# Moving the sums of y to GpSimd, new planner costs for VectorE, and a float64 conversion by 256 columns with its results in place

## The chip, the cores and the metric

The kernel runs on one NeuronCore of one Trainium2 chip. The metric is the device time of one execution in microseconds (us). The names of the engines are those of the profile: PE is TensorE (PEld its weight loads), DVE is VectorE, ACT is ScalarE, POOL is GpSimd, SP is SyncE, which only issues DMAs here. Every engine works its own queue in order: an instruction that waits holds up all that stand behind it in its queue.

## The reference, cut to what matters

Three stages follow each other: a delta-rule attention, a soft mixture of eight experts, and a two-branch product with two more matrices.

```python
y = attention(q, k, v, beta)            # 4 x 8 heads, 768 tokens, state 48 x 48
x = y laid out as (3072, 384)
P = sinkhorn(exp(x @ w_gate))           # (3072, 8)
for e in range(8):                      # w1: (8, 384, 1024)  w2: (8, 1024, 384)
    h = np.maximum(x @ w1[e], 0.0)
    out += P[:, e:e+1] * (h @ w2[e])
a = out @ W1; b = out @ W2              # these weights are float64
result = ((a * b) @ W3) @ W_out         # (3072, 384)
```

## The kernel before

All products are made in three PE passes on split operands: a float32 operand is kept as a high part (rounded by ACT to the PE's fp32r format) and a low part (operand minus high part, also fp32r), and a product is high·high + high·low + low·high. So for each tile of weights and each tile of activations somebody makes a high part (ACT) and a low part (a subtraction, on DVE or POOL).

The program has three phases. Phase A (0 to about 510 us) is the attention with expert 0 beside it. Phase B (to about 1916 us) does experts 1 to 7 for all tokens: three passes over two chunks of 512 tokens, and in each pass 7 experts times 2 halves of the hidden width. One such half is a *unit*; there are 42. Phase C does the last two stages with the converted float64 weights. The change touches phase B alone, and the conversion that runs beside it.

A unit (method `unit`) is 138 matmuls of 128x512: 66 for `x @ w1`, in a scheme in the manner of Strassen that needs sums of weights and sums of token chunks, and 72 for `h @ w2`. The results of the first part come out of PSUM by `hold` (ACT copies a partial sum into `rt`) and `done` (DVE adds PSUM to `rt`, ACT makes the rectified high part `hB` or `hA`, DVE the low part). The second part makes six results y. DVE multiplies each y in PSUM by its expert's probabilities into `tmp` (a ring of two buffers), and a second instruction adds `tmp` to `acc`. That addition is what the title calls the sum of y.

While a unit runs, `load_pair` prepares the weights of the next one, two pairs per unit: four DMAs bring a pair into `rawB` (two buffers, so that one pair fills it), ACT makes the high parts (`wA`, 768 and 640 columns), DVE or POOL the low parts, then five small sums of 128 columns are made within `rawB`, and of three of the sums again high and low parts (`wS`, 256 columns twice, and `wA`, 128 columns). Only then is `rawB` free for the next pair's DMAs.

The float64 weights of the last stage are converted on the way (`convert`), at the lowest priority: by jobs of `CN` columns a DMA brings the raw words into `cvr`, DVE and ACT take exponent and mantissa apart into `cv`, two instructions of DVE or POOL put them together, DVE clears what is too small, ACT makes the high part and DVE or POOL the low part, in `cvs`, and two DMAs store these into DRAM (`w1_d`, `w2_d`, `wo_d`, `w3_d`). There is one `cv` and one `cvs`.

After the fourth expert's first half in each pass, `add_first` brings in expert 0's results from DRAM: six instructions multiply them by the probabilities in `tmp`, six add them to `acc`.

The order of all of it is made by a planner (class `Plan`). Every operation gets a priority, the engines that may do it, and a cost on each. The planner plays the program through with these costs and emits the instructions in that order. Where two engines may do an operation it takes the one that would end it first, where DVE's cost counts 1.5 times (`BIAS`). So a cost is not only a length: it decides the engine and each later place in the queues. `act(n)`, `dve(n)` and `pool2(n)` are the costs in us for n columns; `pool2` is `(2.2 * n + 70) / 1000`.

## Time and profile before

| | us |
|---|---|
| median of three runs | 2279.29 (2276.01 to 2284.38) |
| the profiled execution's own time | 2278.97 |
| its span, first to last instruction | 2277.2 |

The profile is of one execution, and all durations below come from it. The span is 1.77 us shorter than that execution's own time. Busy shares over the whole span are PE 94%, PEld 80%, DVE 73%, ACT 38%, POOL 25%. These are averages over phases with different limits: in phase B DVE is at 82 to 89%, in phase C at a quarter. So the phases are read apart, by stretches of time.

### The profile page before, as it was taken

Reading aid. Unit: us, or ns where it says so; the run is one execution under the profiler, and the core shown is the slowest. Engines: PE = TensorE matmul, PEld = TensorE weight load, DVE = VectorE, ACT = ScalarE, POOL = GpSimd, SP = SyncE. Lnnn points to the kernel's source line nnn. Section 1 sums busy time; section 2 is a strip of 40 time slices with the busy share of each in tenths; the row PEclk is TensorE's granted clock in tenths of the full one; section 3 lists DMA queues with packets and bytes.
Section 4 is the critical chain, followed back from the end, with each engine's and each line's share of the span. In section 5 each row is a group of like instructions: output and inputs, shape, how many; then the busy total and the mean of one; then the engine's idle time right before and its main releaser. Section 6 shows DMA issues by size and latency. Waiting matters only on the chain.

```text
span 2277.2 us, 41249 instructions
## 1 busy us (share of the span) xinstructions
PE 2148.3 (94%) x16017; PEld 1812.5 (80%) x16017; DVE 1653.9 (73%) x3128; ACT 864.6 (38%) x1795; POOL 568.3 (25%) x682
## 2 busy tenths in 40 slices
PE   3989999989999999999999999999999999999999
PEld 3989999987777777777777777777777888888888
DVE  7667866678898999988889989989978666122211
ACT  3333233344434444444434444445433432122222
POOL 3000000033333433343234423423323222300000
PEclk6899999999999999999999999999999999999999
DMA  5331232143224333342323232432322215600000
GB/s 190 90 89 46 86 93 60 32 120 111 82 84 130 93 98 87 89 135 79 92 81 111 84 100 84 131 94 79 88 83 72 65 51 166 134 28 28 15 14 28
DMA packets 228132, 194.90 MB, mean 86 GB/s; under 512 B 17056, under 2 KB 211552, under 8 KB 227168
## 3 DMA queue, kind: packets, MB, share of 16 engines
...
q8 instruction: 125, 2.05, 0.4%
...
## 4 chain that ended last, share of the span: by engine, by line
PE 54%; DVE 22%; issue 8%; DMA 7%; ACT 5%; POOL 3%; SPq 1%; DVEq 0%; POOLq 0%; ACTq 0%
PE b L323 54%; DMA rawB<-in_moe_w 4%; DVE wA L334 2%; DVE hB L337 2%; DVE rt L334 2%; DVE hA L337 2%; DVE cv L337 2%; DVE tmp L334 2%; DVE acc L334 2%; DVE rawB L334 1%; SPq L354 1%; ACT wA L327 1%; DVE wS L334 1%; DVE cv L1192 1%; DVE cv L1196 1%
## 5 line engine op out<-in xcount | busy, mean ns | idle before, releaser
L323 PE MATMUL b<-hB,wA 128*128 128x512 f32 x2277 | 587.9, 398 | 9.2 <-DVE hB L337 9.2
L323 PEld LDWEIGHTS b<-hB,wA 128*128 128x128 f32 x2277 | 429.9, 189 | 119.9 <-DVE hB L337 17.9
L323 PE MATMUL b<-hA,wA 128*128 128x256 f32 (+1 forms) x1611 | 334.2, 338 | 21.1 <-DVE hA L337 19.5
L334 DVE TENSOR_TENSOR rt<-b,rt 128x512 f32<-128x512 f32 x300 | 202.7, 684 | 192.1 <-PE b L323 190.3
L323 PE MATMUL b<-xr,wA 128*128 128x256 f32 (+1 forms) x1620 | 322.0, 336 | 0.0
L323 PEld LDWEIGHTS b<-hA,wA 128*128 128x128 f32 x1611 | 248.5, 191 | 65.8 <-DVE hA L337 31.7
L323 PEld LDWEIGHTS b<-xr,wA 128*128 128x128 f32 x1620 | 251.3, 192 | 32.1
L334 POOL TENSOR_TENSOR wA<-rawB,wA 128x640 fp32r<-128x640 f32 (+2 forms) x117 | 161.2, 1377 | 389.2 <-ACT wA L327 320.5
L323 PE MATMUL b<-xT,wA 128*128 128x512 f32 x1008 | 250.5, 390 | 0.0
L327 ACT ACTIVATE rt<-b 128x512 f32<-128x512 f32 x300 | 176.4, 592 | 139.2 <-PE b L323 122.2
L323 PEld LDWEIGHTS b<-xT,wA 128*128 128x128 f32 x1008 | 189.1, 188 | 40.7
L327 ACT ACTIVATE wA<-rawB 128x768 fp32r<-128x768 f32 (+2 forms) x252 | 155.7, 624 | 147.1 <-PE b L323 76.4
L323 PE MATMUL b<-xT,wS 128*128 128x512 f32 x756 | 204.8, 397 | 7.0 <-ACT wS L327 2.7
L334 DVE TENSOR_TENSOR tmp<-b,pb 128x512 f32<-128x512 f32 x234 | 160.5, 686 | 64.4 <-PE b L323 62.3
L334 DVE TENSOR_TENSOR acc<-acc,tmp 128x512 f32<-128x512 f32 x240 | 180.9, 754 | 4.9
L323 PEld LDWEIGHTS b<-xT,wS 128*128 128x128 f32 x756 | 143.5, 190 | 41.4 <-ACT wS L327 3.6
L327 ACT ACTIVATE cvs<-cv 128x128 fp32r<-128x128 f32 x136 | 42.2, 310 | 349.3 <-DVE cv L337 329.3
L337 DVE SCALAR_TENSOR_TENSOR hB<-rt,hB 128x512 fp32r<-128x512 f32 x170 | 146.8, 868 | 21.4 <-ACT hB L1009 19.6
L334 POOL TENSOR_TENSOR rawB<-rawB 128x128 f32<-128x128 f32 x224 | 132.9, 596 | 108.7 <-DVE rawB L334 51.9
L1009 ACT ACTIVATE hB<-rt 128x512 fp32r<-128x512 f32 x170 | 106.3, 629 | 89.4 <-DVE rt L334 87.8
L334 POOL TENSOR_TENSOR cv<-cv 128x128 f32<-128x128 f32 x118 | 72.9, 618 | 220.9 <-DVE cv L1196 136.3
L334 DVE TENSOR_TENSOR wA<-rawB,wA 128x768 fp32r<-128x768 f32 (+2 forms) x135 | 114.2, 846 | 18.4 <-ACT wA L327 17.5
...
## 6 DMA issues: line engine op xcount, KB each, us to landing
...
w_d<-cvs SPq DMA_DIRECT2D x224, 64.0 KB, 2.3
...
```

The costliest lines, as they stand in the source:

```text
L323: self.nc.tensor.matmul(*args, skip_group_check=True, **kw)
L327: self.nc.scalar.activation(out=out, in_=in_, func=AF.Copy, **({} if scale is None else {"scale": scale}))
L334: self.E[eng].tensor_tensor(out=out, in0=in0, in1=in1, op=op)
L337: self.nc.vector.scalar_tensor_tensor(out=out, in0=in0, scalar=scalar, in1=in1, op0=op0, op1=op1)
L354: return self.g.op({eng: cost}, lambda _: e.dma_start(out=out(), in_=in_()), r=r, w=w, prio=prio, nbytes=nbytes, lat=lat)
L1009: g.op({"ACT": act(512)}, lambda e: nc.scalar.activation(out=hv(0), in_=tv(), func=AF.Relu), r=[t], w=[(out, 0, 0)], prio=pe)
L1192: g.op({"DVE": dve(m)}, lambda e, f=f, rv=rv: ts(out=f(), in0=rv()[:, :, 1], scalar1=3, scalar2=0x3FFFFFF8, op0=ALU.logical_shift_left, op ...
L1196: g.op({"DVE": dve(m, 2)}, lambda e, f=f, ee=ee: ts(out=ee(), in0=f(), scalar1=-0x800000, scalar2=None, op0=ALU.bitwise_and), r=[(cv, "f") ...
```

## The change

Four things are changed, all in phase B and the conversion.

First, the additions to `acc` (in `unit` and `add_first`) may only go to POOL. Second, there are new cost functions for ACT and DVE (`actb`, `dveb`), used throughout phase B; and where DVE and POOL compete for weights' low parts, weights' sums and conversion steps, DVE's cost is doubled (`BB`). Third, a conversion job is 256 columns wide instead of 128, with one raw buffer of twice the width instead of two. Fourth, the conversion's high and low parts no longer have a tile of their own: they are written over the parts of `cv` that held exponent and mantissa, so that the next job's first instruction must wait until the stores have read them.

```diff
-CN = 128
+CN = 256
+BB = 2.0
+def actb(n):
+    return (n / 1.2 + 155) / 1000
+def dveb(n, pair=False):
+    return (n * (1.25 if pair else 1.0) + 140) / 960
...
 # load_pair: low parts, sums, low parts of sums
-            g.op({"POOL": pool2(m), "DVE": dve(m)}, lambda e, n=n, rv=rv, c0=c0: self.tt(
+            g.op({"POOL": pool2(m), "DVE": BB * dveb(m, True)}, lambda e, n=n, rv=rv, c0=c0: self.tt(
...
-            g.op({"POOL": pool2(128), "DVE": dve(128)}, lambda e: self.tt(e, k(*out), k(*i0), k(*i1), op), r=[], w=[(r1, 0), (r2, 0)], prio=prio)
+            g.op({"POOL": pool2(128), "DVE": BB * dveb(128, True)}, lambda e: self.tt(e, k(*out), k(*i0), k(*i1), op), r=[], w=[(r1, 0), (r2, 0)], prio=prio)
...
 # unit (and the same in add_first)
-                    g.op({"POOL": pool2(512), "DVE": dve(512)}, lambda e, tv=tv, av=av: self.tt(e, av(), av(), tv(), ALU.add),
+                    g.op({"POOL": pool2(512)}, lambda e, tv=tv, av=av: self.tt(e, av(), av(), tv(), ALU.add),
...
 # phase_b
-            self.open("cvp", "right", cv=((128, 3, CN), F32), cvr=((128, 2, 2 * CN), F32), rt=((128, 4, 512), F32))
-            self.open("cvs", "right", cvs=((128, 2, CN), F32R))
+            self.open("cvp", "right", cv=((128, 3, CN), F32R), cvr=((128, 1, 2 * CN), F32), rt=((128, 4, 512), F32))
...
 # convert
-        cvraw = Ring([0, 1])
+        cvraw = Ring([0])
...
-            hi = lambda m=m: T["cvs"][:, 0, 0:m]
-            lo = lambda m=m: T["cvs"][:, 1, 0:m]
+            hi = lambda m=m: T["cv"][:, 0, 0:m]
+            lo = lambda m=m: T["cv"][:, 1, 0:m]
...
-            g.op({"ACT": act(m)}, lambda e, hi=hi, r=r: self.copy("ACT", hi(), r()), r=[(cv, "r")], w=[(cv, "h")], prio=pr)
-            g.op({"POOL": pool2(m), "DVE": dve(m)}, lambda e, hi=hi, lo=lo, r=r: self.tt(e, lo(), r(), hi().bitcast(F32),
-                 ALU.subtract), r=[(cv, "r"), (cv, "h")], w=[(cv, "l")], prio=pr)
+            g.op({"ACT": actb(m)}, lambda e, hi=hi, r=r: self.copy("ACT", hi(), r()), r=[(cv, "r")], w=[(cv, "f"), (cv, "h")], prio=pr)
+            g.op({"POOL": pool2(m), "DVE": BB * dveb(m, True)}, lambda e, hi=hi, lo=lo, r=r: self.tt(e, lo(), r(), hi().bitcast(F32),
+                 ALU.subtract), r=[(cv, "r"), (cv, "h")], w=[(cv, "e"), (cv, "l")], prio=pr)
```

Counted over the whole order, DVE goes from 3130 instructions to 2039 and POOL from 687 to 1269. Additions to `acc` on POOL: 12 before, 252 now. Weights' low parts of 768 columns on POOL: 25 before, 84 now; of 640: 54 and 78; sums of 128 columns: 224 and 349; `wS`: 50 and 145. Conversion jobs: 136 before, 72 now. PE's matmuls in phase B are the same, and alternate between the two parts of a unit as before.

The first place is POOL's queue in the middle of phase B, while conversions run. Before, one unit stands in it like this (`wA`, `rawB` and `wS` are a pair's low parts and sums, `cv` and `cvs` conversion steps):

```order
L334 TENSOR_TENSOR wA<-rawB,wA 128x640
L334 TENSOR_TENSOR rawB<-rawB 128x128 x3
L334 TENSOR_TENSOR cv<-cv 128x128
L334 TENSOR_TENSOR wA<-rawB,wA 128x768
L334 TENSOR_TENSOR rawB<-rawB 128x128 x4
L334 TENSOR_TENSOR cv<-cv 128x128
L334 TENSOR_TENSOR wA<-rawB,wA 128x128
L334 TENSOR_TENSOR cvs<-cv,cvs 128x128
L334 TENSOR_TENSOR cv<-cv 128x128 x2
```

After the change a unit begins like this at the same stage. The first nine rows are the pair that is prepared while PE does `x @ w1`; the next 768 belongs to the other pair, whose DMAs may only start once the row above it is done.

```order
L343 TENSOR_TENSOR wA<-rawB,wA 128x768
L343 TENSOR_TENSOR wA<-rawB,wA 128x640
L343 TENSOR_TENSOR cv<-cv 128x256
L343 TENSOR_TENSOR rawB<-rawB 128x128
L343 TENSOR_TENSOR cv<-cv 128x256
L343 TENSOR_TENSOR rawB<-rawB 128x128 x4
L343 TENSOR_TENSOR cv<-cv 128x256
L343 TENSOR_TENSOR wS<-rawB,wS 128x256 x2
L343 TENSOR_TENSOR wA<-rawB,wA 128x128
L343 TENSOR_TENSOR wA<-rawB,wA 128x768
L343 TENSOR_TENSOR wA<-rawB,wA 128x640
L343 TENSOR_TENSOR cv<-cv 128x256
```

Behind these rows stand, to the unit's end: six additions to `acc`, and between them three sums, one `wS`, one `wA` of 128 columns and five conversion steps; the unit ends with addition, two steps, addition, step, addition, all behind the pair's last row. In all a unit has 14 instructions in this queue before and 32 after. The rows shown return word for word in four units (of the first 25); in the others there are 4 to 8 conversion steps, and from the 26th unit on none.

The second place is DVE's queue during `h @ w2` of the same stage. Before, each product into `tmp` has its addition to `acc` behind it, and a pair's low part of 768 columns follows the last:

```order
L1196 TENSOR_SCALAR cv<-cv 128x128
L334 TENSOR_TENSOR tmp<-b_129,pb 128x512
L334 TENSOR_TENSOR cv<-cv 128x128
L334 TENSOR_TENSOR acc<-acc,tmp 128x512
L1204 TENSOR_SCALAR cv<-cvr 128x128
L337 SCALAR_TENSOR_TENSOR cv<-cv 128x128
L334 TENSOR_TENSOR cvs<-cv,cvs 128x128
L334 TENSOR_TENSOR tmp<-b_133,pb 128x512
L334 TENSOR_TENSOR acc<-acc,tmp 128x512
L334 TENSOR_TENSOR wA<-rawB,wA 128x768
L334 TENSOR_TENSOR rt<-b_128,rt 128x512
```

After the change:

```order
L343 TENSOR_TENSOR tmp<-b_134,pb 128x512
L343 TENSOR_TENSOR wS<-rawB,wS 128x256
L1199 TENSOR_SCALAR cv<-cvr 128x256
L343 TENSOR_TENSOR tmp<-b_129,pb 128x512
L346 SCALAR_TENSOR_TENSOR cv<-cvr,cv 128x256
L1203 TENSOR_SCALAR cv<-cv 128x256
L343 TENSOR_TENSOR tmp<-b_130,pb 128x512
L1211 TENSOR_SCALAR cv<-cvr 128x256
L346 SCALAR_TENSOR_TENSOR cv<-cv 128x256
L343 TENSOR_TENSOR tmp<-b_128,pb 128x512
L343 TENSOR_TENSOR rt<-b_133,rt 128x512
```

The additions and the large low part are gone from DVE. What is left between the products are one sum of 128 columns, and the conversion steps, which wait for POOL's.

The third place is POOL's queue in the unit that carries `add_first`, in the first pass. Before:

```order
L334 TENSOR_TENSOR wA<-rawB,wA 128x640
L334 TENSOR_TENSOR rawB<-rawB 128x128
L334 TENSOR_TENSOR tmp<-tmp,rt 128x512
L334 TENSOR_TENSOR rawB<-rawB 128x128
L334 TENSOR_TENSOR cv<-cv 128x128
L334 TENSOR_TENSOR wS<-rawB,wS 128x256
L334 TENSOR_TENSOR acc<-acc,tmp 128x512
L334 TENSOR_TENSOR cvs<-cv,cvs 128x128
L334 TENSOR_TENSOR acc<-acc,tmp 128x512 x2
L334 TENSOR_TENSOR wA<-rawB,wA 128x640
```

After the change:

```order
L343 TENSOR_TENSOR wA<-rawB,wA 128x768
L343 TENSOR_TENSOR tmp<-tmp,rt 128x512 x2
L343 TENSOR_TENSOR acc<-acc,tmp 128x512 x2
L343 TENSOR_TENSOR wA<-rawB,wA 128x640
L343 TENSOR_TENSOR tmp<-tmp,rt 128x512
L343 TENSOR_TENSOR rawB<-rawB 128x128
L343 TENSOR_TENSOR acc<-acc,tmp 128x512
L343 TENSOR_TENSOR tmp<-tmp,rt 128x512
L343 TENSOR_TENSOR rawB<-rawB 128x128
L343 TENSOR_TENSOR acc<-acc,tmp 128x512
L343 TENSOR_TENSOR tmp<-tmp,rt 128x512
L343 TENSOR_TENSOR acc<-acc,tmp 128x512
```

Expert 0's six products and six additions now stand here beside the unit's own six, between the steps of a pair of weights.

## Rows read from the trace of the kernel before

**Rows 1.** The page's busy times of the whole span (busy us, share, instructions).

```profile
PE 2148.3 (94%) x16017; PEld 1812.5 (80%) x16017; DVE 1653.9 (73%) x3128; ACT 864.6 (38%) x1795; POOL 568.3 (25%) x682
```

**Rows 2.** Busy time by stretches: 25 units, 16 units, a quiet one, one wait.

```profile
core 0: us, PE busy (x) PEld busy (x) DVE busy (x) ACT busy (x) POOL busy (x), PEclk, DMA share, GB/s
520.60:1385.10 864.50, 821.16 (x3458) 647.65 (x3457) 770.74 (x1599) 373.79 (x817) 317.17 (x402) 0.99 0.33 96
1385.10:1916.00 530.90, 516.90 (x2200) 415.15 (x2200) 437.06 (x821) 220.91 (x454) 167.44 (x200) 0.99 0.30 88
1800.00:1900.00 100.00, 99.89 (x434) 80.95 (x433) 70.42 (x118) 37.38 (x71) 23.11 (x27) 1.00 0.25 61
759.00:763.00 4.00, 3.70 (x10) 2.94 (x11) 3.06 (x6) 1.73 (x4) 2.89 (x3) 0.57 0.46 130
```

**Rows 3.** Waits in phase B: who for whom, total us, times, longest.

```profile
ACT wS L327 <- POOL rawB L334: 54.9, 38, 2.6
...
PE b L323 <- ACT rt L327: 21.3, 25, 4.1
...
PE b L323 <- DVE hA L337: 19.5, 28, 2.9
...
PE b L323 <- DVE hB L337: 9.2, 14, 1.3
```

**Rows 4.** Groups by shape in phase B (busy us, mean ns | idle before).

```profile
L334 DVE TENSOR_TENSOR acc<-acc,tmp 128x512 f32<-128x512 f32 x235 | 177.4, 755 | 4.7
...
L337 DVE SCALAR_TENSOR_TENSOR hB<-rt,hB 128x512 fp32r<-128x512 f32 x165 | 143.3, 874 | 20.9 <-ACT hB L1009 19.1
...
L334 POOL TENSOR_TENSOR rawB<-rawB 128x128 f32<-128x128 f32 x219 | 130.6, 598 | 105.7 <-DVE rawB L334 51.9 <-DVE wA L334 38.5 <-issue 4.5
...
L334 POOL TENSOR_TENSOR wA<-rawB,wA 128x640 fp32r<-128x640 f32 x54 | 89.8, 1662 | 293.7 <-ACT wA L327 231.2 <-PE b L323 62.6
...
L334 DVE TENSOR_TENSOR wA<-rawB,wA 128x768 fp32r<-128x768 f32 x57 | 70.4, 1234 | 15.1 <-ACT wA L327 14.5 <-issue 0.4
...
L334 DVE TENSOR_TENSOR rawB<-rawB 128x128 f32<-128x128 f32 x191 | 65.9, 354 | 9.8 <-POOL rawB L334 5.2 <-POOL wA L334 3.1
...
L334 DVE TENSOR_TENSOR wS<-rawB,wS 128x256 fp32r<-128x256 f32 x116 | 60.4, 538 | 9.8 <-ACT wS L327 9.4
...
L1204 DVE TENSOR_SCALAR cv<-cvr 128x128 int32<-128x128 int32 x135 | 49.1, 364 | 0.6 <-POOL cv L334 0.4
L334 DVE TENSOR_TENSOR cv<-cv 128x128 f32<-128x128 f32 x153 | 48.1, 314 | 13.5 <-POOL cv L334 6.8
...
L334 POOL TENSOR_TENSOR wS<-rawB,wS 128x256 fp32r<-128x256 f32 x48 | 40.2, 839 | 44.2 <-ACT wS L327 33.4 <-DVE tmp L334 9.7 <-DVE rt L334 0.8
```

**Rows 5.** Timeline in an add_first unit: start, us, what, [idle before].

```profile
1237.34 1.73 POOL L334 TENSOR_TENSOR acc<-acc,tmp 128x512 f32<-128x512 f32 x1
...
1237.85 1.37 DVE L334 TENSOR_TENSOR rawB<-rawB 128x128 f32<-128x128 f32 x1
...
1246.59 0.96 DVE L334 TENSOR_TENSOR wA<-rawB,wA 128x768 fp32r<-128x768 f32 x1
...
1249.27 1.57 POOL L334 TENSOR_TENSOR wA<-rawB,wA 128x640 fp32r<-128x640 f32 x1
...
1254.24 1.29 POOL L334 TENSOR_TENSOR acc<-acc,tmp 128x512 f32<-128x512 f32 x1
1255.49 0.46 POOL L334 TENSOR_TENSOR rawB<-rawB 128x128 f32<-128x128 f32 x1
...
1277.41 0.74 POOL L334 TENSOR_TENSOR wS<-rawB,wS 128x256 fp32r<-128x256 f32 x1 [0.34 <-ACT wS L327]
```

**Rows 6.** Timeline: a low part on each engine, one reload of rawB.

```profile
1092.56 1.88 POOL L334 TENSOR_TENSOR wA<-rawB,wA 128x640 fp32r<-128x640 f32 x1 [3.46 <-ACT wA L327]
1092.93 2.33 DVE L334 TENSOR_TENSOR wA<-rawB,wA 128x768 fp32r<-128x768 f32 x1
...
1100.43 0.28 DVE L334 TENSOR_TENSOR wA<-rawB,wA 128x128 fp32r<-128x128 f32 x1
...
1101.29 1.97 SPq L354 DMA_DIRECT2D rawB<-in_moe_w  x4
...
1105.02 0.85 ACT L327 ACTIVATE wA<-rawB 128x768 fp32r<-128x768 f32 x1 [1.97 <-DMA rawB<-in_moe_w]
...
1105.99 1.85 POOL L334 TENSOR_TENSOR wA<-rawB,wA 128x768 fp32r<-128x768 f32 x1 [6.45 <-ACT wA L327]
1106.41 1.98 DVE L337 SCALAR_TENSOR_TENSOR hB<-rt,hB 128x512 fp32r<-128x512 f32 x1 [1.44 <-ACT hB L1009]
```

**Rows 7.** The page's DMA issues (count, KB each, us to landing).

```profile
w_d<-cvs SPq DMA_DIRECT2D x224, 64.0 KB, 2.3
```

More of the change, by code (lines that the diff above doesn't have):

```diff
@@ L836, in load_pair @@
         raws = []
-        both = {"POOL": pool2(768), "DVE": dve(768)}
         for j, n in enumerate((n1, n1 + 1)):
@@ L869, in load_pair @@
                                  (128, lambda: T["rawB"][:, r1.at, 256:384], lambda i: self.wb(n1 + 1)[:, 768 * i:768 * i + 128], lambda i: ("w", sl2, i))):
-            g.op({"ACT": act(m)}, lambda e, src=src, dst=dst: self.copy("ACT", dst(0), src()), r=rk + ["bopen"], w=[key(0)], prio=prio)
-            g.op({"POOL": pool2(m), "DVE": dve(m)}, lambda e, src=src, dst=dst: self.tt(e, dst(1), src(), dst(0).bitcast(F32), ALU.subtract),
+            g.op({"ACT": actb(m)}, lambda e, src=src, dst=dst: self.copy("ACT", dst(0), src()), r=rk + ["bopen"], w=[key(0)], prio=prio)
+            g.op({"POOL": pool2(m), "DVE": BB * dveb(m, True)}, lambda e, src=src, dst=dst: self.tt(e, dst(1), src(), dst(0).bitcast(F32), ALU.subtract),
                  r=rk + [key(0)], w=[key(1)], prio=prio)
@@ L927, in forms @@
         rk = [("xraw", s, st) for s in range(2) for st in range(2)]
-        both = {"POOL": pool2(512), "DVE": dve(512)}
+        both = {"POOL": pool2(512), "DVE": dveb(512, True)}
         four = lambda v: v.rearrange("p (h t) -> p h t", t=128)
@@ L1001, in hold @@
                 t = temps[q, nm] = self.rt.new()
[L1002 removed]
+                g.op({"ACT": actb(512)}, lambda e: self.copy("ACT", T["rt"][:, t.at], self.ps(s, 512)), r=[s], w=[t], prio=pe)
             def done(nm, s, out):
@@ L1075, in add_first @@
                          [("y0", 2 * ch + st, kk) for st in range(2)], [tm], pr)
-                g.op({"POOL": pool2(512), "DVE": dve(512)}, lambda e, tv=tv, bv=bv: self.tt(e, tv(), tv(), bv(), ALU.mult), r=[b], w=[tm], prio=pr)
+                g.op({"POOL": pool2(512), "DVE": BB * dveb(512, True)}, lambda e, tv=tv, bv=bv: self.tt(e, tv(), tv(), bv(), ALU.mult), r=[b], w=[tm], prio=pr)
                 av = lambda s=s, kk=kk: T["acc"][:, s, kk]
-                g.op({"POOL": pool2(512), "DVE": dve(512)}, lambda e, tv=tv, av=av: self.tt(e, av(), av(), tv(), ALU.add), r=[tm],
+                g.op({"POOL": pool2(512)}, lambda e, tv=tv, av=av: self.tt(e, av(), av(), tv(), ALU.add), r=[tm],
                      w=[("acc", s, kk)], prio=pr)
@@ L1197, in convert @@
                  op0=ALU.bitwise_and), r=[(cv, "f")], w=[(cv, "e")], prio=pr)
-            g.op({"ACT": act(m)}, lambda e, r=r, rv=rv: nc.scalar.activation(out=r(), in_=rv()[:, :, 0].bitcast(U32), func=AF.Copy,
+            g.op({"ACT": actb(m)}, lambda e, r=r, rv=rv: nc.scalar.activation(out=r(), in_=rv()[:, :, 0].bitcast(U32), func=AF.Copy,
                  scale=2.0 ** -52), r=[raw], w=[(cv, "r")], prio=pr)
-            g.op({"POOL": pool2(m), "DVE": dve(m)}, lambda e, r=r, ee=ee: self.tt(e, r(), r(), ee().bitcast(F32), ALU.mult),
+            g.op({"POOL": pool2(m), "DVE": BB * dveb(m, True)}, lambda e, r=r, ee=ee: self.tt(e, r(), r(), ee().bitcast(F32), ALU.mult),
@@ L1201, in convert @@
                  r=[(cv, "e")], w=[(cv, "r")], prio=pr)
-            g.op({"POOL": pool2(m), "DVE": dve(m)}, lambda e, r=r, f=f: self.tt(e, r(), r(), f().bitcast(F32), ALU.add),
+            g.op({"POOL": pool2(m), "DVE": BB * dveb(m, True)}, lambda e, r=r, f=f: self.tt(e, r(), r(), f().bitcast(F32), ALU.add),
                  r=[(cv, "f")], w=[(cv, "r")], prio=pr)
-            g.op({"DVE": dve(m)}, lambda e, ee=ee, rv=rv: ts(out=ee(), in0=rv()[:, :, 1], scalar1=0x7FFFFFFF, scalar2=None,
+            g.op({"DVE": dveb(m)}, lambda e, ee=ee, rv=rv: ts(out=ee(), in0=rv()[:, :, 1], scalar1=0x7FFFFFFF, scalar2=None,
```

29 lines of the change are left out of this document (14 added, 15 removed).

## The prediction

> **What bounds the kernel now.** I read the page's busy times first, then busy times by stretches, then the waits of phase B, then groups by shape, and at last single instructions in the timeline.
>
> PE is busy 94% of the span [rows 1], so only its idle time and its slow stretches can be won. I cut phase B where units begin their second part, into 25 units (520.6 to 1385.1 us) and 16 units (to 1916.0): the matmul counts 3458 and 2200 are 25.1 and 15.9 times 138 [rows 2]. The first 25 take 864.5 us, 34.6 each; the others 530.9 us, 33.2 each. In the quiet stretch 434 matmuls take 99.89 us, so a unit that waits for nothing takes 138 x 0.230 = 31.8 us. PE's idle time is 43.3 and 14.0 us in the two stretches, 57.3 us together; the granted clock of 0.99 over 1395 us is another 14 us or so [rows 2]. So a change confined to phase B can win 71 us at most, if every wait goes.
>
> The waits that PE has there are for ACT's `rt` (21.3 us), DVE's `hA` (19.5) and DVE's `hB` (9.2) [rows 3]. They stand behind other work on those engines: DVE is busy 89% of the first stretch and 82% of the second, POOL only 37% and 32% [rows 2]. POOL comes in indirectly: ACT waits 54.9 us for POOL's sums in `rawB` before it can make `wS` [rows 3], and what stands behind that in ACT's queue waits too.
>
> **What VectorE gives up.** The 235 additions in these stretches are 177.4 us. Of low parts of 768 columns all 59 go (x 1.234 = 73 us), of sums 125 (x 0.354 = 44 us), of `wS` 95 (x 0.538 = 51 us) [rows 4]. Conversion: 72 jobs instead of 136, each twice as wide. Its instructions at 128 columns take about 0.31 to 0.36 us [rows 4]; at 256 they cost between the same and double, so the total is between 0.53 and 1.06 of today's. The nearest row is `wS` at 256 against a sum at 128, 0.538 to 0.354, a factor of 1.5, so 0.8 of today's 270 us: 55 us saved. Together 400 us of the 1208 that DVE is busy in the two stretches: it falls from 87% to about 58%. ACT saves fixed cost on the same jobs, and SP issues 192 fewer DMAs; both were off the path, so I count nothing.
>
> **What GpSimd takes on.** This is where I put the sum. Undisturbed, POOL's instructions take 1.29 us (addition), 0.46 (sum of 128), 0.74 (`wS`, 256) [rows 5], 1.57 (640) [rows 5] and 1.85 (768) [rows 6]. A conversion step of 256 columns isn't in the trace; it has the shape of `wS`, so 0.74, and cannot be under the 0.46 of 128 columns or over twice that, 0.92.
>
> The unit whose rows the change shows has 6 additions (7.7), two 768 (3.7), two 640 (3.1), 8 sums and 2 of `wA` 128 (4.6), 3 `wS` and 9 conversion steps (8.9): 28.0 us. To this comes idle time that the order forces. A pair fills `rawB`, so the next pair's DMAs start when the last low part is done: from 1100.71 to POOL's next 768 at 1105.99 it took 5.3 us [rows 6]. Twice per unit POOL meets this. Behind the second pair stand three additions and three steps, 6.1 us, which hide it; behind the first pair's last row the next 768 follows at once, so 5.3 us are idle. 33.3 us, and PE needs 31.8. A lighter unit (6 additions, 3 + 2 conversion steps, 9 sums) is 25.0 us of work, and 1.75 and 2.8 us of it stand in the two reloads, so 3.5 and 2.5 us idle: 31.0 us.
>
> Then the port. A POOL addition takes 1.29 us alone and 1.73 beside a DVE instruction with two operands in SBUF [rows 5]; a DVE low part takes 0.96 alone [rows 5], 2.33 beside POOL's [rows 6]. On average POOL's instructions are 0.09 to 0.14 us longer than undisturbed (0.598 to 0.46, 1.662 to 1.57, 0.839 to 0.74) [rows 4 to 6]. With a third of DVE's work gone I take 0.09 per instruction; the ends are 0 and 0.2. So 32 x 0.09 = 2.9 us for the heavy unit and 2.6 for the light one: 36.2 and 33.6 us. Both are over PE's 31.8.
>
> The Trainium skill ("SBUF — State Buffer", section "Who interferes with whom") says that the port pair shared by VectorE and GpSimd is an exclusive lock held for the whole instruction. The rows agree in kind: 1092.93 + 2.33 ends 0.8 us after POOL's 640 at 1094.44, so DVE hardly moved meanwhile. It speaks against this change, since it makes GpSimd's and VectorE's shares of the port add up; that is the third rival below.
>
> **The sum.** Counted along the new order of the first 25 units: four heavy ones at 36.2 (145 us); thirteen in between, which come to 33.2 to 35.4 by the same working, mean 34.4 (447); five so light that PE bounds them, at 32.0 (160); one with the token sums of a new pass, 44; and two with `add_first`. Those have 13 additions and 6 products (19 x 1.29 = 24.5), 6.8 of low parts, 8 short instructions and 9 of 256 columns (10.3), 1.8 idle and 40 x 0.09: 47 each (94). Total 890, less 3 that the light units behind the new pass make up: 887 against 864.5, +22.5 us. The last 16 have no conversion: 14 at 32.0, one `add_first` at 44, one new pass at 35, less 5 of slack before and behind them: 522 against 530.9, -9 us. A late unit shows as one wait of PE of 2 to 4 us, and waits of that length drop the clock: in 759 to 763 us, behind a wait of PE, it was 0.57, between the levels of 1.2 and 2.4 GHz, for 4 us [rows 2], 1.7 us lost. I add six of these, +10 us. Sum: +23.5 us. The profiled execution took 2278.97 us (1.77 over its span; the median of the runs is 2279.29), so 2302 us.
>
> Results in place: a conversion's first instruction now waits for the stores, 2.3 us to landing [rows 7]. It has no deadline before phase C and ends with the 25th unit, so I count 0; DVE's slack of 40% hides it. If it falls where PE waits for DVE, a tenth of 72 x 2.3 us is 17 us. A gain is excluded, since nothing waits for the conversion.
>
> **Rivals.**
>
> VectorE was the limit. For it: half of PE's waits are for DVE's `hA` and `hB`, DVE is at 89% and POOL at 37% [rows 2, 3]; an addition has two buffers before PE feels it, weights a unit's time. If POOL's lateness is swallowed, two thirds of the 71 us go: 2232 us. Against it: POOL's own sum per unit, over 31.8 us in 20 of 25 units, which no slack swallows for long.
>
> The two cancel. If the port costs half of what I take (0.045 us), the heavy unit is 34.7, the middle ones 33.0, the other terms shrink likewise: 858 and 522 us, no clock term, -15; with 10 us of waits for POOL's sums before `wS` in ACT's queue that is 2274 us.
>
> The port serves one at a time. DVE's instructions in a heavy unit that want it are six low parts of `h` (0.874 each) and 15 conversion instructions of 0.3 to 0.4 [rows 4]: about 10 us, so 38 us with POOL's 28, and some of the reload's idle time on top; an average conversion unit comes to 37.5. 22 x 37.5 + 3 x 47 = 966, +100 us with everything else as above: 2380 us. For it: DVE's 1.98 us at 1106.41, right where PE waited for `hB` [rows 6]. Against it: the mean of these is 0.874, not 1.98 [rows 4].
>
> **Chances and range.** Forecast 0.49; VectorE was the limit 0.25; they cancel 0.17; the port 0.09. The price at the port decides most: by the same sum 0.07 us per instruction gives 2287 and 0.13 gives about 2335, which is the forecast's own range; 0 (every unit near PE's 32 us) gives 2242 and 0.2 about 2380, which are the rivals' ground. For 8 in 10 it must reach well into the first rival and somewhat toward the last: 2238 to 2360 us. A measurement of this kernel tells a change of about 0.5%, 11 us. Faster by more: 0.26 (the first rival and a sliver of the second). Within: 0.21 (the second, and the forecast's low end). Slower: 0.53.
>
> **What would show it.** Right: in the first stretch POOL busy over 85%, DVE under 70%, periods of 34 to 37 us where nine conversion steps stand in a unit, PE waiting for ACT or DVE that themselves waited for POOL, and 32 us per unit after the conversion ends. Wrong: POOL with regular idle time in front of its additions (waiting for DVE's products) in the first 25 units, a mean addition on POOL near 1.3 us, and PE's idle time there under 43 us. The forecast falls as a whole if the two-buffer ring and the unit of lead let PE run at 32 us although POOL is late; then the sum over POOL's queue was the wrong place to look.

## The result and the profile after

The changed kernel takes 2315.83 us (median of four runs, 2305.11 to 2319.72), the kernel before 2281.07 in the same set: a ratio of 1.0147, 95% interval 1.0107 to 1.0186, so 34.8 us slower. The forecast was 2302 us, slower, with a range of 2238 to 2360. The profiled execution of the changed kernel is the slowest of the four, 2319.72 us with a span of 2318.0.

The 40.8 us between the two spans lie in these places (units begin with their second part, as in the prediction). The matmul number 8000, up to which the order of every engine's work is the same in both kernels, comes at 446.9 us before and at 455.8 after: 8.9 us that differ from one execution to the next (over all runs below it comes between 437.1 and 457.6). From there to the first unit 73.7 became 79.2, +5.5. The first 25 units take 903.5 us instead of 864.5, +39.0; the last 16 take 518.0 instead of 530.9, -12.9; what follows 361.5 instead of 361.2.

The page's busy times, beside [rows 1]:

```profile
PE 2153.9 (93%) x16017; PEld 1822.8 (79%) x16017; DVE 1436.1 (62%) x2037; ACT 843.5 (36%) x1664; POOL 1233.7 (53%) x1264
```

Busy time by stretches, the same 25 and 16 units as in [rows 2]:

```profile
535.00:1438.50 903.50, 826.59 (x3452) 653.66 (x3451) 699.57 (x972) 369.39 (x756) 750.22 (x779) 0.97 0.32 100
1438.50:1956.50 518.00, 510.96 (x2200) 414.27 (x2199) 294.60 (x374) 205.61 (x387) 376.90 (x383) 0.99 0.25 73
```

POOL went from 317 to 750 us in the first stretch (83% of it) and from 167 to 377 in the second. DVE gave back only 71 and 142 us: it is busy 77% and 57%, in the mean 70% where 58% was forecast. PE's idle time is 76.9 us in the first stretch (43.3 before) and 7.0 in the second (14.0).

The waits of phase B (who for whom, total us, times, longest), beside [rows 3]:

```profile
ACT cv L336 <- DVE cv L346: 231.1, 50, 8.5
...
ACT wS L336 <- POOL rawB L343: 117.5, 53, 7.6
...
PE b L332 <- ACT rt L336: 73.7, 35, 11.3
...
PE b L332 <- DVE hB L346: 1.4, 4, 0.7
...
PE b L332 <- DVE hA L346: 0.7, 1, 0.7
```

and one of the kernel before that stands beside the first:

```profile
ACT cvs L327 <- DVE cv L337: 328.5, 121, 7.4
```

The waits for DVE's `hA` and `hB` are nearly gone, the wait for ACT's `rt` has grown from 21.3 to 73.7 us, and ACT's own wait for POOL's sums from 54.9 to 117.5. Of these 117.5 us only 49.3 lie in the first stretch (40.5 before), where the time was lost. There ACT's wait for the reload of `rawB` has grown too, from 48.8 to 89.9 us. ACT stands for 231 us in front of a conversion's rounding, which waits for DVE; that was 328.5 us in 121 waits before, so its total is no cause, but a single one can be.

The groups by shape of both stretches (busy us, mean ns of one | idle time before), beside [rows 4]:

```profile
L343 POOL TENSOR_TENSOR acc<-acc,tmp 128x512 f32<-128x512 f32 x246 | 332.3, 1353 | 57.4 <-DVE tmp L343 55.1
...
L343 POOL TENSOR_TENSOR rawB<-rawB 128x128 f32<-128x128 f32 x339 | 189.6, 566 | 19.8 <-DVE rawB L343 7.1
...
L343 DVE TENSOR_TENSOR rt<-b,rt 128x512 f32<-128x512 f32 x246 | 166.6, 683 | 64.2 <-PE b L332 34.1 <-ACT rt L336 28.4 <-ACT wA L336 0.5
L346 DVE SCALAR_TENSOR_TENSOR hB<-rt,hB 128x512 fp32r<-128x512 f32 x166 | 166.2, 1007 | 61.0 <-ACT hB L1017 59.2
L343 DVE TENSOR_TENSOR tmp<-b,pb 128x512 f32<-128x512 f32 x228 | 155.6, 683 | 113.9 <-PE b L332 102.5 <-POOL acc L343 10.3 <-POOL wA L343 1.1
...
L343 POOL TENSOR_TENSOR wA<-rawB,wA 128x640 fp32r<-128x640 f32 x76 | 126.6, 1666 | 9.8 <-ACT wA L336 7.9 <-PE b L332 1.9
L343 POOL TENSOR_TENSOR wS<-rawB,wS 128x256 fp32r<-128x256 f32 x141 | 119.3, 861 | 6.1 <-ACT wS L336 4.3
...
L343 DVE TENSOR_TENSOR rawB<-rawB 128x128 f32<-128x128 f32 x71 | 64.9, 914 | 28.4 <-POOL wA L343 25.4 <-POOL rawB L343 3.0
...
L346 DVE SCALAR_TENSOR_TENSOR cv<-cvr,cv 128x256 int32<-128x256 int32 x62 | 60.0, 969 | 1.2
...
L1211 DVE TENSOR_SCALAR cv<-cvr 128x256 int32<-128x256 int32 x62 | 39.1, 631 | 21.8 <-POOL cv L343 21.4
```

and of the kernel before:

```profile
L334 DVE TENSOR_TENSOR rt<-b,rt 128x512 f32<-128x512 f32 x246 | 165.4, 682 | 8.7 <-PE b L323 6.9 <-ACT rt L327 1.3
```

POOL's instructions cost what was forecast: the sum of 128 columns 0.566 us, `wS` 0.861, an addition 1.353, each 0.06 to 0.12 over its undisturbed time. DVE's are what has changed: a sum on `rawB` 0.914 instead of 0.354, `hB` 1.007 instead of 0.874, and the conversion's instructions at 256 columns 0.57 to 0.97 us, 1.7 to 2.8 times those of 128. Two rows of the same size as `hB` did not move at all: `rt` and `tmp`, which read PSUM (`b`), take 0.683 us, and took 0.682 and 0.686 before.

Two places show how this reaches PE. The first is in a unit with nine conversion steps (timeline: start, us, engine, line, what, idle before it and what ended it):

```profile
1199.56 1.65 POOL L343 TENSOR_TENSOR cv<-cv 128x256 f32<-128x256 f32 x2
...
1200.33 0.29 DVE L1211 TENSOR_SCALAR cv<-cvr 128x256 int32<-128x256 int32 x1 [1.27 <-POOL cv L343]
...
1201.18 1.28 POOL L343 TENSOR_TENSOR acc<-acc,tmp 128x512 f32<-128x512 f32 x1
1201.25 1.49 DVE L346 SCALAR_TENSOR_TENSOR cv<-cv 128x256 f32<-128x256 int32 x1 [0.63 <-POOL cv L343]
...
1202.77 0.42 ACT L336 ACTIVATE cv<-cv 128x256 fp32r<-128x256 f32 x1 [6.78 <-DVE cv L346]
1203.10 0.83 ACT L336 ACTIVATE wA<-rawB 128x768 fp32r<-128x768 f32 x1
...
1203.83 0.58 ACT L336 ACTIVATE rt<-b 128x512 f32<-128x512 f32 x1
...
1204.46 1.65 PE L332 MATMUL b<-xT,wS 128*128 128x512 f32 x6 [2.23 <-ACT rt L336]
```

Read it from the end. PE stands 2.23 us until ACT's `rt` copy is done. That copy stands in ACT's queue behind a copy of weights, `wA`, and behind a conversion's rounding, `cv`, and this waited 6.78 us for DVE. DVE's instruction there took 1.49 us; alone it takes 0.41. It ran from 1201.25, beside POOL's addition from 1201.18. Before it DVE had twice waited for POOL's conversion steps, 1.27 and 0.63 us, so a part of ACT's wait is POOL's lateness, as the forecast had it. The two `cv` instructions have no deadline; what stands behind them has.

The second is the new unit of `add_first`:

```profile
767.53 1.95 DVE L346 SCALAR_TENSOR_TENSOR cv<-cvr,cv 128x256 int32<-128x256 int32 x1
...
769.16 2.72 POOL L343 TENSOR_TENSOR tmp<-tmp,rt 128x512 f32<-128x512 f32 x2
...
770.68 1.74 DVE L346 SCALAR_TENSOR_TENSOR hA<-rt,hA 128x512 fp32r<-128x512 f32 x1
771.84 3.10 POOL L343 TENSOR_TENSOR acc<-acc,tmp 128x512 f32<-128x512 f32 x2
...
772.35 2.88 DVE L343 TENSOR_TENSOR cv<-cv 128x256 f32<-128x256 f32 x2
772.52 0.60 ACT L336 ACTIVATE rt<-b 128x512 f32<-128x512 f32 x1 [4.62 <-DVE hA L346]
...
775.86 0.63 ACT L1017 ACTIVATE hB<-rt 128x512 fp32r<-128x512 f32 x1 [2.74 <-DVE rt L343]
...
779.14 1.08 ACT L336 ACTIVATE rt<-b 128x512 f32<-128x512 f32 x2 [0.51 <-DVE hB L346]
...
779.79 1.65 PE L332 MATMUL b<-xr,wS 128*128 128x512 f32 x3 [10.03 <-ACT rt L336]
```

POOL runs one 512-column instruction after the other, each again beside DVE's. DVE's conversion instruction took 1.95 us and the low part `hA` 1.74 (0.68 alone); ACT waited 4.62 us for `hA` to give back a buffer of `rt`. Two more of DVE's conversion instructions, 2.88 us beside POOL's additions, stand in front of the sum into `rt` that ACT waits for next (2.74 us). The copy that PE needs starts at 779.14, and PE has waited 10.03 us.

### The profile page after: what moved, and what is told of

It reads as the page before. It is cut to its first block, busy times and chain, and to the rows that moved or that the text cites. A ratio compares the mean times of both kernels' runs of the same rounds, so it can differ in the third digit from the quotient of the medians.

```text
span 2318.0 us, 40182 instructions
## 1 busy us (share of the span) xinstructions
PE 2153.9 (93%) x16017; PEld 1822.8 (79%) x16017; DVE 1436.1 (62%) x2037; ACT 843.5 (36%) x1664; POOL 1233.7 (53%) x1264
## 4 chain that ended last, share of the span: by engine, by line
PE 55%; POOL 14%; DVE 11%; DMA 9%; issue 6%; ACT 4%; SPq 1%; DVEq 0%; POOLq 0%; ACTq 0%
PE b L332 55%; DMA rawB<-in_moe_w 3%; POOL rawB L343 3%; POOL acc L343 3%; POOL cv L343 3%; POOL wA L343 2%; DVE cv L346 2%; POOL wS L343 2%; DMA w_d<-cv 2%; SPq L363 1%; DVE hB L346 1%; DVE cv L1199 1%; DVE tmp L343 1%; DMA xst<-xs_d 1%; ACT wA L336 1%
## 5 line engine op out<-in xcount | busy, mean ns | idle before, releaser
L332 PE MATMUL b<-hB,wA 128*128 128x512 f32 x2277 | 580.1, 395 | 1.5 <-DVE hB L346 1.4
L343 POOL TENSOR_TENSOR wA<-rawB,wA 128x768 fp32r<-128x768 f32 (+2 forms) x228 | 326.2, 1439 | 171.1 <-ACT wA L336 169.1
L343 POOL TENSOR_TENSOR acc<-acc,tmp 128x512 f32<-128x512 f32 x252 | 340.0, 1351 | 67.7 <-DVE tmp L343 65.4
L332 PE MATMUL b<-xr,wA 128*128 128x256 f32 (+1 forms) x1620 | 327.6, 340 | 0.0
L332 PE MATMUL b<-hA,wA 128*128 128x256 f32 (+1 forms) x1611 | 326.0, 335 | 0.8 <-DVE hA L346 0.7
L332 PE MATMUL b<-xT,wS 128*128 128x512 f32 x756 | 215.0, 410 | 32.9 <-ACT rt L336 25.0
L346 DVE SCALAR_TENSOR_TENSOR hB<-rt,hB 128x512 fp32r<-128x512 f32 x170 | 169.5, 1003 | 62.6 <-ACT hB L1017 60.8
L343 POOL TENSOR_TENSOR rawB<-rawB 128x128 f32<-128x128 f32 x349 | 194.5, 564 | 20.4 <-DVE rawB L343 7.1
L343 POOL TENSOR_TENSOR cv<-cv 128x256 f32<-128x256 f32 (+3 forms) x172 | 136.3, 792 | 40.2 <-DVE cv L1203 14.8
L343 POOL TENSOR_TENSOR wS<-rawB,wS 128x256 fp32r<-128x256 f32 x145 | 122.8, 861 | 7.6 <-ACT wS L336 5.5
```

Of the source, the lines that this page charges most:

```text
L332: self.nc.tensor.matmul(*args, skip_group_check=True, **kw)
L343: self.E[eng].tensor_tensor(out=out, in0=in0, in1=in1, op=op)
L346: self.nc.vector.scalar_tensor_tensor(out=out, in0=in0, scalar=scalar, in1=in1, op0=op0, op1=op1)
```

## The experiments

Stretches are measured as above; "steps" are conversions begun in the first 25 units (of 72 with `CN` 256, of 136 with 128), DVE and POOL the busy us there. Ratios are to the kernel before in the same set of runs; its median was 2274.7 to 2281.1 us over these sets, so times of different sets are compared better by their ratios.

| kernel | us | ratio, 95% | 25 units | steps | DVE, POOL | 16 units |
|---|---|---|---|---|---|---|
| before | 2281.1 | | 864.5 | 102 n | 771, 317 | 530.9 |
| after | 2315.8 | 1.0147 [1.0107, 1.0186] | 903.5 | 70 | 700, 750 | 518.0 |
| acconly | 2318.2 | 1.0182 [1.0162, 1.0201] | 885.1 | 100 n | 776, 467 | 548.1 |
| convonly | 2299.7 | 1.0102 [1.0077, 1.0128] | 889.1 | 70 | 750, 438 | 520.2 |
| bb1 | 2307.8 | 1.0122 [1.0087, 1.0157] | 890.0 | 70 | 741, 631 | 522.9 |
| accboth | 2303.6 | 1.0123 [1.0080, 1.0165] | 893.2 | 70 | 742, 664 | 520.6 |
| first_dve | 2308.8 | 1.0151 [1.0123, 1.0178] | 899.9 | 70 | 705, 718 | 518.8 |
| conv_dve | 2352.6 | 1.0321 [1.0288, 1.0353] | 944.8 | 70 | 809, 632 | 518.1 |
| noconv | 2264.3 | 0.9945 [0.9921, 0.9968] | 848.2 | (64) | 445, 587 | 522.6 |
| noadd | 2250.8 | 0.9873 [0.9841, 0.9906] | 855.1 | 70 | 605, 583 | 514.9 |
| spread | 2285.1 | 1.0036 [1.0009, 1.0062] | 853.9 | 46 | 618, 672 | 546.7 |
| convonly_spread | 2279.6 | 1.0001 [0.9981, 1.0022] | 849.2 | 45 | 689, 355 | 535.7 |
| before_spread | 2295.4 | 1.0080 [1.0049, 1.0111] | 864.8 | 84 n | 728, 296 | 546.3 |
| accboth_bb1_spread | 2271.3 | 0.9960 [0.9942, 0.9979] | 847.2 | 46 | 670, 481 | 536.1 |

n: steps of 128 columns. (64): their loads, one instruction of ACT and the stores alone.

**One part alone: the additions (acconly).** The kernel before, with both `acc` additions on POOL:

```diff
-g.op({"POOL": pool2(512), "DVE": dve(512)}, ... av(), av(), tv(), ALU.add)
+g.op({"POOL": pool2(512)}, ... av(), av(), tv(), ALU.add)
```

> The kernel before with one part of the change alone: the additions of y are made on GpSimd only (252 of them, before 12); costs and conversion as before. By its order GpSimd's instructions of phase B (low parts, sums, conversion, additions) come to 741 us instead of 464, 17.6 us per unit, with 5.3 us of a reload 23. Theory Q (the period of a unit is GpSimd's own sum): 23 is far under PE's 31.8 us, so this part alone costs nothing, and VectorE gives up some 195 us: 2255 to 2281 us. Rival P (the port: every GpSimd instruction slows VectorE's low parts of h, and PE waits for these): 252 more instructions that meet VectorE, so slower than before, 2290 to 2310. Rival V (VectorE was the limit before): two thirds of 71 us go, about 2235.

As slow as the whole change, with POOL at 53% of the first stretch. Q falls here: 23 us of POOL per unit cannot fill 31.8. Windows of the two stretches, and two groups of the first:

```profile
519.70:1404.80 885.10, 824.34 (x3452) 650.70 (x3450) 776.33 (x1493) 369.42 (x814) 467.16 (x498) 0.98 0.31 93
1404.80:1952.90 548.10, 523.35 (x2205) 415.41 (x2206) 415.23 (x741) 221.30 (x457) 282.17 (x289) 0.99 0.29 86
```

```profile
L334 POOL TENSOR_TENSOR acc<-acc,tmp 128x512 f32<-128x512 f32 x150 | 211.9, 1419 | 134.0 <-DVE tmp L334 132.5
...
L337 DVE SCALAR_TENSOR_TENSOR cv<-cvr,cv 128x128 int32<-128x128 int32 x100 | 86.4, 864 | 1.7
```

141 additions, 107 us, left DVE there, and it is as busy as before (776 us; 771 in [rows 2]): the conversion's instruction on two SBUF operands went from 0.348 to 0.864 us. P foresaw the sign and was 8 us short of the size; V falls, for what DVE gave away came back to it as waiting.

**Another part alone: the conversion (convonly).** The kernel before with `CN = 256`, results in `cv`, one raw buffer instead of two, and the new costs of its instructions, the doubled one included.

> The kernel before with another part alone: the conversion by 256 columns with its results in place, at the measured costs; additions and low parts as before. GpSimd's instructions of phase B come to 568 us by the order (13.5 us per unit). Theory Q: GpSimd is far from the bound, so 2270 to 2290 us, no difference. Rival W (width and results in place are what costs: in the changed kernel VectorE's conversion instructions took 0.57 to 0.97 us at 256 columns, against 0.29 to 0.35 at 128): slower by most of the 34 us, 2300 to 2315, and the instructions at 256 take 0.6 us or more here too.

The time comes out at the edge of W's range, but not in W's way: the wide instructions take 0.36 to 0.58 us beside a POOL that is busy half the time. What is new is in the idle time before two of them. The kernel before, then this one, first stretch:

```profile
L1198 ACT ACTIVATE cv<-cvr 128x128 f32<-128x128 uint32 x102 | 31.8, 312 | 23.8 <-DVE cvs L334 12.3 <-POOL cvs L334 10.5 <-DMA cvr<-in_w3T 1.0
...
L1192 DVE TENSOR_SCALAR cv<-cvr 128x128 int32<-128x128 int32 x101 | 28.9, 286 | 0.0
```

```profile
L1200 DVE TENSOR_SCALAR cv<-cvr 128x256 int32<-128x256 int32 x62 | 35.9, 579 | 45.0 <-DMA w_d<-cv 27.9 <-DMA cvr<-in_moe_w 6.0 <-DMA cvr<-in_w3T 5.4
...
L1206 ACT ACTIVATE cv<-cvr 128x256 f32<-128x256 uint32 x62 | 26.6, 429 | 78.5 <-DMA cvr<-in_w3T 39.0 <-DMA cvr<-in_moe_w 32.0 <-DMA cvr<-in_moe_w_out 6.6
```

DVE now waits 45 us for the stores of the last step and the next load before a step's first instruction, and ACT's read 78.5 us, most of it for the load, which has only one buffer to go to. What stands behind them waits too:

```profile
1009.88 0.44 ACT L1206 ACTIVATE cv<-cvr 128x256 f32<-128x256 uint32 x1 [2.02 <-DMA cvr<-in_w3T]
...
1010.23 0.58 ACT L336 ACTIVATE rt<-b 128x512 f32<-128x512 f32 x1
...
1010.86 1.44 PE L332 MATMUL b<-xT,wS 128*128 128x512 f32 x5 [1.39 <-ACT rt L336]
```

The `rt` copy that PE needs is in ACT's queue behind a read that waits for its DMA. That separate buffers would mend this was not tried.

**A number undone (bb1).** The changed kernel:

```diff
-BB = 2.0
+BB = 1.0
```

> The changed kernel with one number undone: BB is 1 instead of 2, so low parts, sums and steps are planned at VectorE's measured time and not at twice that. By its order GpSimd's instructions come to 959 us instead of 1166, 22.8 us per unit; VectorE takes the rest. Theory Q: with 5.3 us of reload and 2.5 us of port a mean unit is 31 us, under PE's 31.8 in most units; the loss of the 25 units falls from 39 us to 5 to 15 and the time to 2275 to 2295 us. Rivals P and W (the port or the wide conversion on VectorE): VectorE gets more to do and is slowed as before, so no gain: 2305 to 2325.

```profile
518.00:1408.00 890.00, 825.07 (x3445) 651.44 (x3445) 740.78 (x1093) 364.91 (x753) 630.69 (x659) 0.98 0.33 102
```

119 us less of POOL in the first stretch than in the changed kernel, and 13.5 us won there; the median is in P's range. The profiled execution, 2293.3 us, is the fastest of four.

**The other part undone (accboth).** The changed kernel with the additions allowed on both engines:

```diff
-g.op({"POOL": pool2(512)}, ... av(), av(), tv(), ALU.add)
+g.op({"POOL": pool2(512), "DVE": dveb(512, True)}, ... av(), av(), tv(), ALU.add)
```

> The changed kernel with one part undone: the additions of y may go to either engine again; conversion and doubled costs as changed. By its order 214 of the 270 go to VectorE, GpSimd's work falls from 1166 to 949 us, 22.6 us per unit, about as in bb1, where low parts were moved instead. Theory Q (GpSimd's own queue): 22.6 + 5.3 us of reload + 2.5 us of port is 30.4, under PE's 31.8: 2275 to 2290 us. Theory J (both engines' undisturbed durations add up at the port): an addition asks 0.68 us of it on VectorE and 1.28 on GpSimd, so 128 us less in phase B, some 860 instead of 939 us in the first 25 units, where runs with 843 to 885 us took 854 to 890: 2280 to 2305. Theory D (VectorE is late again as soon as it gets more to do): no gain, 2310 to 2330.

2303.6 us: over Q, at the upper end of J. The expectation's 22.6 us of POOL are a mean of all 42 units; in the first 25 it is 26.6, so here Q was not tested far under its limit (in bb1 it is 25.2). With bb1 it shows that a ninth to a sixth of POOL's load, given to DVE, moves the first stretch by 10 to 14 of the 39 us.

**The lump (first_dve).** The changed kernel with `add_first` on DVE:

```diff
-g.op({"POOL": pool2(512), "DVE": BB * dveb(512, True)}, ... tv(), tv(), bv(), ALU.mult)
+g.op({"DVE": dveb(512, True)}, ... tv(), tv(), bv(), ALU.mult)
-g.op({"POOL": pool2(512)}, ... av(), av(), tv(), ALU.add)
+g.op({"DVE": dveb(512, True)}, ... av(), av(), tv(), ALU.add)
```

> The changed kernel with the products and additions of add_first (12 instructions in each of three places) on VectorE alone; all else as in the changed kernel. In the changed kernel these units took 46.7, 48.3 and about 45 us. Theory Q: GpSimd gives up 12 x 1.4 = 17 us there, and these units come to 35 to 39 us: 20 to 30 us are won, 2286 to 2298 us. Rival S (the slack of a unit's lead hides such a lump, and what counts is the mean load in every unit): under 8 us won, 2308 or more.

The two units take 45.7 and 45.4 us instead of 46.7 and 48.3. The median is S's, but the test was weaker than it was meant to be: where the twelve instructions stood in POOL's queue, the plan puts a third pair's low parts and sums, and POOL is busy 36.8 and 34.9 us in the two units instead of 38.9. So these two do not decide between Q and S. The third such unit, behind the conversion, does more: in the changed kernel it takes 36.7 us (and not the 45 of the expectation), and here 38.0, though POOL is busy 25.9 us instead of 30.7. The lump is now in DVE's queue, in front of the same low part `hA`:

```profile
765.34 1.06 DVE L343 TENSOR_TENSOR tmp<-tmp,rt 128x512 f32<-128x512 f32 x1 [1.97 <-DMA tmp<-y_d]
...
766.32 1.62 DVE L1199 TENSOR_SCALAR cv<-cvr 128x256 int32<-128x256 int32 x1
767.86 0.68 DVE L343 TENSOR_TENSOR acc<-acc,tmp 128x512 f32<-128x512 f32 x1
...
768.46 0.94 DVE L346 SCALAR_TENSOR_TENSOR hA<-rt,hA 128x512 fp32r<-128x512 f32 x1
...
769.49 0.60 ACT L336 ACTIVATE rt<-b 128x512 f32<-128x512 f32 x1 [4.90 <-DVE hA L346]
```

**The conversion on DVE (conv_dve), the conversion left out (noconv), the additions left out (noadd).** The changed kernel with

```diff
-g.op({"POOL": pool2(m), "DVE": BB * dveb(m, True)}, ...)    # three steps
+g.op({"DVE": dveb(m, True)}, ...)
-g.op({"ACT": actb(m)}, ... self.copy("ACT", hi(), r()) ...)
+g.op({"DVE": dveb(m)}, ... self.copy("DVE", hi(), r()) ...)
```

> The changed kernel with three steps and the rounding of each conversion on VectorE alone; ACT keeps only the read of the raw words. GpSimd's work of phase B falls from 1166 to 1039 us, VectorE gets some 190 instructions more. Theory H (head of line: a conversion step has no deadline, but it stands in ACT's and GpSimd's queues in order and waits there for VectorE, 6.78 us at one place of ACT, with copies and weights that PE needs behind it): these waits are gone, the first 25 units take 870 us or less instead of 903.5, the time 2275 to 2290 us. Theory Q (GpSimd's load sets the period): 3 us less per unit, 2295 to 2305. Theory P (the port: VectorE's instructions wait for GpSimd's): VectorE gets more to do beside a GpSimd nearly as busy: 2315 to 2335.

> The changed kernel with the arithmetic of the conversion left out, except for the one instruction of ACT; its DMAs stay. GpSimd's work 1023 us, about that of conv_dve. Theory H: 835 to 855 us in the first 25 units, 2250 to 2270 us. Theory Q: as conv_dve, 2293 to 2303, since GpSimd has the same to do. Theory P: VectorE gives up 300 us that it now spends on the conversion: 2265 to 2285.

> The changed kernel with the additions of y in the units left out (234 of 252; the 18 of add_first stay). GpSimd's work falls from 1166 to 892 us, 21 us per unit. Theory H: the conversion still stands in the queues, so little is won: 2300 to 2312 us. Theory Q: every unit is under PE's 31.8 us, the first 25 take 850 us: 2265 to 2280. Theory P: 316 us less of GpSimd's instructions in VectorE's way: 2260 to 2285, and the conversion's instructions on VectorE go from 0.57 to 0.97 us to under 0.6.

```profile
529.40:1474.20 944.80, 841.06 (x3451) 665.85 (x3450) 809.49 (x1191) 345.92 (x686) 632.07 (x626) 0.95 0.31 96
```

```profile
529.60:1377.80 848.20, 813.31 (x3452) 651.50 (x3451) 444.64 (x580) 345.24 (x679) 587.14 (x607) 0.99 0.35 103
```

```profile
527.20:1382.30 855.10, 814.82 (x3452) 652.26 (x3451) 605.42 (x926) 369.24 (x755) 583.28 (x685) 0.98 0.35 108
```

conv_dve and noconv have the same work on POOL by the order, and are 88 us apart: Q is out. H is out too: without any conversion in POOL's queue and with only the read in ACT's the time got worse. noadd wins 65 us (62 by the ratios), more than any theory gave; of P's two signs the sign of the time holds, the fall of the instructions to under 0.6 us only in part (`cv` from `cvr` and `cv` 0.969 to 0.623, the last one 0.728 to 0.767). P is left: 37 us slower where DVE gets more beside a busy POOL, faster where either loses work altogether.

**The same work, later (spread).** The changed kernel, with the plan alone altered:

```diff
-            o.est = 0.0
-            o.rdy = dict.fromkeys(o.engs, 0.0)
+            o.est = o.hold
+            o.rdy = dict.fromkeys(o.engs, o.hold)
...
-            self.dma(lambda raw=raw, m=m: T["cvr"] ...
+            o = self.dma(lambda raw=raw, m=m: T["cvr"] ...
+            o.hold = 470.0 + 17.5 * k
```

> The changed kernel with a not-before time in the plan for each conversion's load, 17.5 us apart, so that the 72 conversions are planned over all 41 units (1.75 in each) and not over the first 25 (2.9 in each). The same work in all. If each conversion costs its price wherever it stands (H, P): the first 25 units win what the last 16 lose, 2308 to 2320 us. If a unit has slack for one or two of them and not for three (Q: about 28 us of GpSimd's work in each, none over 31.8): 2280 to 2298 us.

```profile
522.50:1376.40 853.90, 815.03 (x3452) 650.41 (x3451) 617.65 (x854) 355.42 (x707) 672.32 (x704) 0.99 0.30 91
1376.40:1923.10 546.70, 518.31 (x2200) 412.19 (x2199) 377.39 (x519) 221.94 (x436) 422.75 (x436) 0.99 0.31 93
```

24 steps fewer in the first stretch win 49.6 us, 25 more in the second cost 28.7: 30.7 us of the 34.8 are back by the medians, about 25 by the ratios, without one instruction less. The steps do not cost the same everywhere.

**Spread on other bases (convonly_spread, before_spread, accboth_bb1_spread).** The same lines on convonly; on the kernel before, with 9.3 us between its 136 steps; and on the changed kernel with the additions on both engines and BB 1.

> The kernel before with the conversion by 256 columns and its results in place (as in convonly), and its 72 loads planned 17.5 us apart, over all 41 units. Theory J (VectorE's instructions with all operands in SBUF and GpSimd's instructions share one port; what counts is the sum of both, each at its undisturbed duration, in every stretch): the sum over phase B is 1121 us in convonly (797 in the first 25 units, 324 behind them), 27.3 us per unit when spread; units with such a sum took 33 us in the runs so far, so 2245 to 2265 us, faster than before. Theory R (the rate of conversion does nothing by itself, spread only took load from GpSimd): as convonly, 2290 to 2305.

> The kernel before with nothing but its 136 conversion loads planned 9.3 us apart, over all 41 units (before they end in the 33rd or so). Theory J: the sum of both engines is 1154 us in phase B, 756 of it in the first 25 units (30.2 us per unit, period 34.6); spread it is 28.1 in each, so some 33.3 us per unit: 2255 to 2272 us. Theory R: 2272 to 2285, as before.

> The changed kernel with additions allowed on both engines, BB 1 and the conversion's loads planned 17.5 us apart. GpSimd's work 779 us by the order (19 us per unit), VectorE's the rest. Theory J: work that GpSimd takes costs the port nearly twice what it costs on VectorE (1.28 against 0.68 us for an addition), the sum is about 1250 us, 30.5 per unit: 2268 to 2285 us, slower than convonly_spread by 10 us or more. Theory B (a balance of the two engines' busy times is what counts, each being under 60 to 70%): the best of all, 2240 to 2255, faster than convonly_spread.

convonly_spread wins 39.9 us in the first stretch against convonly and gives 15.5 back; the median is 20 us better and equal to the kernel before, its profiled execution reached the first unit 16 us later than that of before, 10.7 of them ahead of matmul 8000. J's figure of 2245 to 2265 is missed, and J falls with before_spread, which it had faster and which is 0.8% slower: 18 narrow steps fewer in the first stretch won nothing there and 18 more in the second cost 15.4 us. Why narrow steps are free in one stretch and dear in the other stays open. accboth_bb1_spread is the fastest complete kernel, 0.4% under the one before; B had the order right and the size wrong.

## Why the prediction was right, and where its reasons were not

**Sign and size.** Slower was the likeliest, and 2315.8 lies in the forecast's own range of 2287 to 2335. Of the terms, +22.5 us for the first 25 units and +10 for the clock came out as +39.0 together: PE's idle time grew by 33.6 us and its busy time, for the same matmuls at a granted clock of 0.97 instead of 0.99, by 5.4. The -9 for the last 16 units came out as -12.9, and the 5.5 us ahead of the first unit had no term. Since the paragraphs below take its main reason apart, it is in good part luck that the sum lands so near.

**Its own signs.** In the first stretch POOL is busy 83% (over 85 was named) and DVE 77% (under 70); both are missed. The 32 us per unit behind the conversion came, and three of four heavy units lie in 34 to 37 us. That PE waits for what waited for POOL holds in part, as in the first place above. Of the signs of being wrong none came: 14.1 us of idle time before POOL's 150 additions there, 1.377 us in the mean of one, PE idle 76.9 us.

**GpSimd's instructions.** Right: 0.1 over undisturbed, where 0.09 was taken. The unit periods look right as well: 36.4, 36.9, 35.3 and 38.8 us for four units with nine steps (36.2), 46.7 and 48.3 with `add_first` (47), 43.4 with the token sums (44), 32.4 in the mean of the last 16 (32). But the third `add_first` unit, among these 16, takes 36.7 where 44 was put.

**GpSimd's own sum as the limit.** This step failed: "POOL's own sum per unit, over 31.8 in 20 of 25 units, which no slack swallows for long". acconly has 18.7 us of POOL in a mean unit of the first stretch and is as slow. In bb1 it is 25.2, with the reload's 5.3 us 30.5, and 25.5 of the 39 us stay; in conv_dve 25.3, and a mean unit takes 37.8. (accboth, with 26.6 and the reload, is at the limit of 31.8 and decides nothing.) In the changed kernel the other 22 units do not follow POOL's busy time either: one takes 39.0 us with 26.7 of it, another 33.1 with 31.3. That 47 met 46.7 was no proof of the sum behind it.

**What VectorE gives up.** The term that was mis-sized: 400 us, measured 214. By each shape's undisturbed time (the 5% point of its durations over the runs) DVE's instructions without a PSUM operand ask for 489 us in the first stretch before and 256 after; their records sum to 619 and 510 (records overlap a little at their ends). So the work fell by 233 us and the waiting rose from 130 to 254. The wide conversion, put at 0.8 of its old time, takes 302 us instead of 295 in phase B, though POOL has most of its steps. I had looked for the price of the port on POOL's instructions only, where it is a tenth of a us, and not on DVE's.

**Results in place.** Counted 0 with a bound of 17 us. In convonly DVE waits 27.9 us for the stores, and ACT 78.5 us, one wait of them in front of PE, mostly for a load into the single raw buffer, for which the sum had no term at all. It costs something; how much of convonly's 21 us was not separated. In the changed kernel ACT's read stands idle for 9.9 us only and DVE 15.6 for the stores, so convonly's price need not be the whole's.

**The rivals.** That VectorE was the limit falls with acconly: relieved of 141 additions it was no freer. The cancelling falls. The port was the nearest mechanism, at the wrong price: 37.5 us were forecast for an average conversion unit and 47 for the other three, 34.8 and 46.1 measured. The instructions that it counted (six low parts and 15 of the conversion) are indeed ones without a PSUM operand; it had no term for the rate.

**What takes the place of the failed step.** Two things go with the time of the first stretch, and no run parts them fully. One is the rate of steps. With 70 wide ones the stretch takes 889 to 904 us in convonly, bb1, accboth, first_dve and after, with POOL busy 438 to 750 us; with 45 or 46 it takes 847 to 854, no more than with none (848); and spread and convonly_spread, which win 49.6 and 39.9 us there, change the plan alone. But the rate is not all: noadd has 70 steps too and takes 855 us, conv_dve 945, and acconly lost 20.6 us with narrow steps at the old rate.

The other is what DVE waits beside POOL, by the working under "What VectorE gives up". With 70 steps it is 168 us in noadd, 238 in bb1, 245 in accboth, 248 in first_dve, 254 in after and 296 in conv_dve, and the time rises in this order: 855, 890, 893, 900, 904, 945. In acconly it is 205, where 130 were before. Only convonly stands apart (160 us of waiting, 889 of time), and it has the waits for its one raw buffer.

How it reaches PE can be followed back from the end of each of PE's waits in the first stretch, by what released an instruction or stood before it in its queue, to the wait's start. In the changed kernel these are 41 waits, 76 us: ACT's work is 33.5 us of it (12.7 before), DVE's conversion instructions 14.5 (1.1 before), DVE's low parts and sums into `rt` 7.2 (18.5 before), and POOL's own work 5.6 (1.8 before). This is the pattern of the two places shown: steps without a deadline end up in front of copies and low parts with one.

Why the plan lets them is argued and was not tried: it takes 0.41 us for one of DVE's conversion instructions, (256 + 140)/960, and 0.63 for one of POOL's, (2.2 x 256 + 70)/1000; beside each other they take 0.57 to 0.97 and 0.80 to 0.85. The parts alone (40 and 21 us) do not add up to the whole (35), and their overlap was not separated.
